# Block-summary scores of an attention stage: two half-width matmuls side by side, or two full-width matmuls that accumulate into one bank

## The chip, the cores and the metric

One core of a Trainium2 chip runs the whole program. The metric is the time of one execution on the device, in microseconds (us). Each kernel was executed several times, and medians are quoted. A ratio is the mean time of one kernel's fast runs over that of the other's fast runs of the same rounds, so it is not quite the ratio of the medians. The granted clock is the share of TensorE's full clock that a run was given. A run counts as slow when it is over 1.5% above the fastest of the same kernel.

## The reference, cut to what matters

An attention stage (4 batches, 8 heads, 768 positions, 64 per head) is followed by a mixture of experts, which takes most of the time. In the attention, each query sees its near keys and, besides, one summary per block of 32 keys, the elementwise maximum of the block:

```python
k_sum = k.reshape(B, H, nb, block, D).max(axis=3)        # nb = 24 blocks
scores_s = scale * np.einsum('bhsd,bhnd->bhsn', q, k_sum)
scores_s = scores_s + np.log(block)
...
a = np.exp(scores_all)
```

The change concerns `scores_s`, a small product: 24 summaries against 768 queries, contraction 64.

## The kernel before: what the change and the argument touch

The kernel works on two heads at a time (a "pair of heads", 16 in all, numbered `i`). Two heads of 64 fill the 128 rows of the matmul array. The maxima of both heads are laid out block-diagonally in `ksT`, so that one matmul gives the summaries of both heads: 64 output partitions (2 heads, 24 blocks padded to 32). As 768 queries don't fit one of the kernel's banks of 512 columns, the queries come in two halves of 384. For the last twelve pairs of heads, both halves go into one bank, one to partitions 0 to 63 and one to 64 to 127:

```python
def key_max_split(i):                      # maxima of both heads, block-diagonal
    nc.vector.tensor_tensor(out=ksT[r][:, 0:64]..., in0=ks[r]..., in1=own..., op=ALU.mult)

def summaries_2(i):
    r, ss = i % NB, bank("a", "ss")
    for h in range(2):                     # h: half of the queries
        at["ss", i, h] = ss[64 * h:64 * h + 64]
        nc.tensor.matmul(ss[64 * h:64 * h + 64, 0:HS], lhsT=ksT[r][:, 0:64],
                         rhs=qT[r][:, W + h * HS:W + (h + 1) * HS], start=True, stop=True)

def summary_exp(i, h):                     # ScalarE, one exponential for each half
    ...
# in the constants, on VectorE, once for each of the four ksT:
nc.vector.memset(t[:, 64:128], 0.0)
```

A planner in the program decides the order of all work on each engine from estimated costs. It fills the attention of later batches with the dense layers of expert 0 (`hps` is its hidden layer, `yps` its output), so that TensorE (PE) always has something to do. Below, "the pair" means the two matmuls of `summaries_2`. Other names in the timelines: `sg` are the scores with the near keys (matmuls of 64 rows), `Ee` the exponentials of the summaries' scores, `av` the attention's result and "the values" the matmuls of line 441 that use `Ee`; `tkq` are transposed queries and keys, `tx` and `xT` the attention's result transposed for the experts, and `lp` the logits of the router that weighs the experts. PEld is TensorE's weight load, DVE is VectorE, ACT is ScalarE.

The softmax here doesn't subtract the row's maximum and nothing guards it: scores larger than these inputs give would overflow.

## Time and profile before

| | |
|---|---|
| time, median of the 6 runs beside the changed kernel | 667.33 us (667.11 to 668.03) |
| span of the profiled execution | 665.9 us |
| TensorE busy | 658.1 us (99%) |
| pairs changed | 12, from 37.0 to 107.1 us |
| from one `hps` matmul's start to the next, 384 columns | 162.5 ns |
| from the pair's first start to the next matmul's start | 286 ns |

The prediction below shows the views. One thing in reading them matters throughout: a matmul's duration in the profile (350 ns here) is longer than the time to the next one's start (162.5 ns in an undisturbed run of the same width), so successive matmuls overlap. What a matmul costs a busy TensorE is the time from its start to the next one's start. I therefore read the single records of the trace for starts in nanoseconds, where a timeline row merges several.

### The profile page before, as it was taken

How to read it: one execution, taken by the hardware profiler on the slowest of the kernel's cores; microseconds unless marked ns; L12 is line 12 of the kernel's file. 1: busy time of each engine (PE TensorE's matmuls, PEld its weight loads, DVE VectorE, ACT ScalarE, POOL GpSimd, SP SyncE). 2: the span in 40 equal slices, each digit the busy share in tenths (PEclk: the TensorE clock that was granted, in tenths of full speed). 3: DMA queues.
4: the chain of work that ended last, by engine and by line, in shares of the span. 5: the costliest groups of instructions: out<-in, count | busy, mean ns of one | idle time of the engine just before them, and what ended most of it. 6: DMA issues, size and time to landing. Idle time of an engine off the chain costs nothing.

```text
span 665.9 us, 13246 instructions
## 1 busy us (share of the span) xinstructions
PE 658.1 (99%) x5132; PEld 434.5 (65%) x5132; DVE 550.3 (83%) x1034; ACT 411.8 (62%) x769; POOL 199.0 (30%) x257
## 2 busy tenths in 40 slices
PE   8999999999999999999999999999999999999997
PEld 4666656555676666666666666666666666666666
DVE  7899977798989887887779877888778877988776
ACT  6677766566875566556665665555655656556652
POOL 8999522100132222212322222213122213222123
PEclk9999999999999999999999999999999999999999
DMA  9999952700763747373754666373838465334656
GB/s 168 183 148 144 136 70 42 127 0 2 134 118 62 123 75 123 66 127 65 110 97 72 119 88 104 64 127 65 127 64 138 69 95 96 64 64 111 155 135 202
DMA packets 112558, 67.89 MB, mean 102 GB/s; under 512 B 77936, under 2 KB 90480, under 8 KB 112496
## 3 DMA queue, kind: packets, MB, share of 16 engines
q0 software_dynamic: 94816, 57.46, 65.3%
q1 hardware_dynamic: 17152, 9.58, 6.2%
q8 instruction: 40, 0.66, 0.4%
q14 instruction: 22, 0.18, 0.1%
q10 hardware_dynamic: 528, 0.02, 0.0%
HBM read 52.45 MB, written 6.29 MB: 88 GB/s over the span
## 4 chain that ended last, share of the span: by engine, by line
PE 93%; DMA 3%; issue 1%; DVE 1%; POOL 0%; ACT 0%; POOLq 0%; DVEq 0%; ACTq 0%
PE yps L815 21%; PE pA L764 21%; PE pY L815 16%; PE pQ L764 10%; PE hps L211 6%; PE yps L216 6%; PE pR L764 5%; DMA out_acc<-y 2%; PE sg L347 1%; PE tkq L303 1%; DMA qst<-in_q_dram 1%; PE vs L357 1%; PE av L435 1%; PE av L512 1%; PE tx L550 1%
## 5 line engine op out<-in xcount | busy, mean ns | idle before, releaser
L815 PEld LDWEIGHTS <-h 128*128 128x128 f16 x2352 | 230.1, 98 | 89.9 <-issue 2.0
L843 POOL DMA_DIRECT2D out_acc<-y x120 | 101.4, 888 | 373.0 <-ACT y L839 107.0
L839 ACT ACTIVATE y<-pY,P_sb 128x256 f32<-128x256 f32 x168 | 80.0, 477 | 126.7 <-PE pY L815 124.0
L830 DVE SCALAR_TENSOR_TENSOR out_acc<-yps,P_sb,out_acc 128x512 f32<-128x512 f32 x128 | 95.3, 745 | 28.0 <-PE yps L815 27.9
L798 DVE TENSOR_TENSOR h<-h 128x1024 f16<-128x1024 f16 x168 | 109.2, 684 | 1.3
L815 PE MATMUL pY<-w,h 128*128 128x256 f16 x672 | 100.3, 273 | 0.6 <-ACT y L839 0.6
L764 PE MATMUL pA<-xT,w 128*128 128x512 f16 x336 | 98.6, 379 | 0.0
L815 PE MATMUL yps<-w2sum,h 128*128 128x256 f16 x672 | 97.9, 273 | 0.0
L815 PE MATMUL yps<-w,h 128*128 128x256 f16 x672 | 93.3, 273 | 0.0
L830 DVE SCALAR_TENSOR_TENSOR out_acc<-pY,P_sb,out_acc 128x512 f32<-128x512 f32 x84 | 62.9, 749 | 29.7 <-PE pY L815 28.1
L764 PEld LDWEIGHTS <-w 128*128 128x128 f16 x672 | 65.8, 98 | 31.3 <-issue 0.2
L764 PEld LDWEIGHTS <-w1sum 128*128 128x128 f16 x504 | 49.3, 98 | 44.6
L786 DVE CUSTOM_DVE_ANT_0 h<-pQ,snap 128x512 f16<-128x512 f32 x84 | 57.7, 686 | 6.5 <-ACT snap L207 3.6
L786 DVE CUSTOM_DVE_ANT_0 h<-pA,snap 128x512 f16<-128x512 f32 x84 | 57.5, 684 | 5.4 <-PE pA L764 5.0
L202 ACT ACTIVATE h<-pA 128x512 f16<-128x512 f32 x84 | 50.6, 603 | 12.1 <-PE pA L764 12.0
L202 ACT ACTIVATE h<-pR 128x512 f16<-128x512 f32 x84 | 50.1, 596 | 8.1 <-PE pR L764 8.1
L815 PE MATMUL pY<-w2sum,h 128*128 128x256 f16 x336 | 50.4, 273 | 0.6 <-ACT y L839 0.5
L207 ACT COPY pR<-pA 128x512 f32<-128x512 f32 x82 | 46.8, 571 | 6.7 <-PE pA L764 5.9
L764 PE MATMUL pA<-xsum,w 128*128 128x512 f16 x168 | 50.0, 379 | 0.0
L764 PE MATMUL pQ<-xsum,w1sum 128*128 128x512 f16 x168 | 50.0, 379 | 0.0
L764 PE MATMUL pR<-xT,w 128*128 128x512 f16 x168 | 50.0, 379 | 0.0
L764 PE MATMUL pQ<-xT,w1sum 128*128 128x512 f16 x168 | 50.0, 379 | 0.0
(150 smaller groups left out, 851.6 us busy)
## 6 DMA issues: line engine op xcount, KB each, us to landing
out_acc<-y POOLq DMA_DIRECT2D x120, 256.0 KB, 3.4
w<-in_moe_w_dram POOLq DMA_DIRECT2D x14, 1024.0 KB, 10.3
out_dram<-out_acc SPq DMA_DIRECT2D x24, 256.0 KB, 2.4
qst<-in_q_dram POOLq DMA_DIRECT2D x32, 96.0 KB, 5.6
vx<-in_v_dram POOLq DMA_DIRECT2D x15, 192.0 KB, 6.4
kst<-in_k_dram POOLq DMA_DIRECT2D x24, 96.0 KB, 5.7
w<-in_moe_w_dram POOLq DMA_DIRECT2D x4, 256.0 KB, 7.0
w<-in_moe_w_dram POOLq DMA_DIRECT2D x2, 512.0 KB, 8.5
```

What stands on the lines that cost most here:

```text
L202: nc.scalar.activation(out=out, in_=in_, func=AF.Relu, bias=0.0, scale=1.0)
L207: (nc.scalar.copy if eng == "ACT" else nc.vector.tensor_copy)(out=out, in_=in_)
L211: nc.tensor.matmul(hp[:, 0:n], lhsT=w1s[e][:, dk, f * 128:(f + 1) * 128], rhs=xT[:, dk, t0:t0 + n], start=(dk == 0), stop=(dk == KD - 1))
L216: nc.tensor.matmul(yp[:, d], lhsT=h[:, f, c * 128:(c + 1) * 128], rhs=w2s[e][:, f, d], start=(f == 0), stop=(f == KF - 1))
L303: nc.tensor.transpose(t[:, g * 128:(g + 1) * 128], st[:, g, :, :].rearrange("p j d -> p (j d)"), ident)
L764: nc.tensor.matmul(dst[:], lhsT=lhsT, rhs=rhs, start=first and k == 0, stop=k == HK - 1, skip_group_check=True)
L786: nc.vector._custom_dve(dve_ops.TENSOR_ADD_SAT, out=ring(e, p, q)[:, q % 2, blk, :], in0=at[src, e, p, q][:], in1=at.pop(("snap", n, e, p, ...
L798: nc.vector.tensor_tensor(out=h[:, :, out_, :], in0=h[:, :, a, :], in1=h[:, :, b, :], op=op)
L815: nc.tensor.matmul(dst[:, d], lhsT=lhsT, rhs=rhs, start=f == 0 and n in (1, 5, 2), stop=f == HF - 1, skip_group_check=True)
L830: nc.vector.scalar_tensor_tensor(out=o, in0=y, scalar=scalar, in1=o, op0=ALU.mult, op1=ALU.add)
L839: nc.scalar.activation(out=at[key][:, d], in_=src, func=AF.Copy, bias=0.0, scale=P_sb[:, t, e:e + 1])
L843: nc.gpsimd.dma_start(out=o, in_=at.pop(("y", e, p, c, key))[:], accum_op=ALU.add)
```

## The change

Its intent: the two narrow matmuls become full-width ones, so that the array never changes its shape for them. `ksT` becomes 192 columns wide, with zeros on both sides of the 64 columns of maxima. The window 64:192 has the maxima first and zeros after, and the window 0:128 has the zeros first. The first matmul puts half 0 on partitions 0 to 63 and zeros on the others. The second adds zeros to those and half 1 to the others.

```diff
-        ksT = [attn.tile([128, 128], BF16, name=f"ksT{i}") for i in range(NB)]
+        ksT = [attn.tile([128, 192], BF16, name=f"ksT{i}") for i in range(NB)]
...
-            nc.vector.tensor_tensor(out=ksT[r][:, 0:64].rearrange("p (j n) -> p j n", j=2),
+            nc.vector.tensor_tensor(out=ksT[r][:, 64:128].rearrange("p (j n) -> p j n", j=2),
...
-            nc.tensor.matmul(ss[:, 0:HS], lhsT=ksT[r][:], rhs=rhs, start=True, stop=True)
+            nc.tensor.matmul(ss[:, 0:HS], lhsT=ksT[r][:, 64:192], rhs=rhs, start=True, stop=True)
...
-                nc.tensor.matmul(ss[64 * h:64 * h + 64, 0:HS], lhsT=ksT[r][:, 0:64],
-                                 rhs=qT[r][:, W + h * HS:W + (h + 1) * HS], start=True, stop=True)
+                nc.tensor.matmul(ss[:, 0:HS], lhsT=ksT[r][:, 64 - 64 * h:192 - 64 * h],
+                                 rhs=qT[r][:, W + h * HS:W + (h + 1) * HS], start=h == 0, stop=h == 1)
...
-                nc.vector.memset(t[:, 64:128], 0.0)
+                nc.vector.memset(t[:], 0.0)
```

The order of instructions stays the same on every engine.

## The prediction

> **What bounds the kernel now.** I read the page first: its busy shares, then the chain that ended last.
>
> ```profile
> PE 658.1 (99%) x5132; PEld 434.5 (65%) x5132; DVE 550.3 (83%) x1034; ACT 411.8 (62%) x769; POOL 199.0 (30%) x257
> ...
> PE 93%; DMA 3%; issue 1%; DVE 1%; POOL 0%; ACT 0%; POOLq 0%; DVEq 0%; ACTq 0%
> ```
>
> TensorE (PE) is busy for 99% of the span and holds 93% of the chain. A busy matmul row is no proof of a full array, because matmuls overlap, so I next asked for the table of stretches and for all waits of PE.
>
> ```profile
> 36.00:72.00 36.00, 36.00 (x454) 23.48 (x451) 33.53 (x89) 28.04 (x45) 35.24 (x42) 1.00 2.36 145
> 72.00:110.00 38.00, 38.00 (x375) 22.48 (x374) 31.15 (x86) 28.79 (x54) 12.73 (x23) 1.00 0.96 83
> ...
> PE pY L815 <- ACT y L839: 1.0, 2, 0.6
> PE tkq L312 <- DMA qst<-in_q_dram: 0.7, 1, 0.7
> ```
>
> The columns of the first two lines are the stretch, its length, then busy us of PE, PEld, DVE, ACT and POOL, the granted clock (1.00, full), and DMA. The changed matmuls (line 461) run from 37.0 to 107.1 us, so both stretches hold all of them: PE never stops there, and its list of waits for them is empty. The waits shown lie before 8 us or after 554 us. In this region the order on PE sets the end: time taken out of PE's stream is time off the kernel, as long as no new wait appears.
>
> The two matmuls themselves, by tile, and then in the timeline of PE around one pair:
>
> ```profile
> L461 PE MATMUL ss<-qT,ksT x24: 350/350/350, 37.0 to 107.1; 128*64 128x384 bf16 x24
> L472 ACT ACTIVATE Ee<-ss x24: 471/487/488, 37.4 to 108.4; 64x384 bf16<-64x384 f32 x24
> ...
> 45.56 0.82 PE L211 MATMUL hps<-xT,w 128*128 128x384 f16 x4
> 46.32 0.35 PE L461 MATMUL ss<-qT,ksT 128*64 128x384 bf16 x2
> 46.60 0.82 PE L211 MATMUL hps<-xT,w 128*128 128x384 f16 x4
> ```
>
> The third line from the end is a run of four full-width matmuls of 384 columns, the second the pair. Its two matmuls take 0.35 us together although each takes 350 ns: in the single records the second starts 4 ns after the first. Each uses half of the array's columns (128\*64), and the halves run side by side. So the pair already costs one matmul's streaming, not two. What matters are its edges: 46.60 - 46.32 = 0.28 us until the next matmul starts. In an undisturbed run of the same width the chain of waits shows
>
> ```profile
> 115.77 1.95 PE hps L211 x12
> ```
>
> that is 1.95 / 12 = 0.1625 us each. The excess is the subject of this prediction.
>
> **What the Trainium skill says.** "TensorEngine Tiling (Array Packing)", section Key Properties: different tiles work in parallel, and changing the tiling mode drains TensorE. The trace agrees on both. I listed, for each change of line on PE, the time from one matmul's start to the next beyond its own streaming. Full-width to full-width: 0 (hps to tkq, yps to av and others), with waits on semaphores or not. Full-width to the 64-column pair: 93 to 94 ns, ten times of ten. Pair to full-width: 286 ns after the pair's first start, against 162.5, so 120 ns beyond the 4 ns of stagger, twelve of twelve. "TensorE: Matmul & The Clock Gate", section Back-to-back issue gap: N/2.4 + 2.5 ns for N columns at full clock; for 384 that is 162.5, which the line above shows exactly. Its section Weight-path perf modes says the fast weight load needs 128 columns; the trace has 106 ns for the 64-column load and 98 ns for a 128-column one, both hidden under streaming, so I give this no weight. "Perfetto Trace Analysis", section Tensor Engine Instruction: PE's end times are modelled; hence I count from start to start.
>
> **The change part by part.** There are twelve pairs (24 matmuls). Their instructions stay in number and order on every engine: the comparison of instruction orders differs only in 24 matmul shapes (64 to 128 columns) and four memsets.
>
> 1. *Removed: the mode switch in, the narrow pair, the switch out.* For a pair behind a full-width matmul (ten of twelve): 94 + 286 = 380 ns until the next matmul starts, and that next one then holds PE 173 ns in place of 162.5, so 11 more: 391 ns.
> 2. *Added: two full-width matmuls one after the other.* They are written to all 128 partitions of one bank and the second adds to the first, as the four hps matmuls of a group do without a gap. 2 x 162.5 = 325 ns. The zero half of the weights costs nothing in itself. Saved: 391 - 325 = 66 ns, ten times, 0.66 us.
> 3. *Two pairs come behind score matmuls of 64 rows* (sg; at 53.8 and 107.1 us). There a switch is paid whatever follows: 90 ns into the pair, 92 to 93 into full width. Before: 90 + 286 + 11 = 387. After: 92 + 325 + 11 = 428. Lost: 41 ns twice, 0.08 us. No pair is followed by a tiled matmul.
> 4. *The maxima* are written to columns 64 to 127 in place of 0 to 63, same shape (216 ns, sixteen times): zero. The h=1 matmuls of the first batch (line 455) read the same 128 columns shifted: zero.
> 5. *Memsets*: four of 128x32 words, at a step of about 42 ns, become 128x96. From 128x64 at a step of 75 ns I estimate about 108, so 0.27 us more on DVE at 2 us. DVE then waits 1.09 us for a load before 7.01 us, so this hides.
>
> Sum on PE: 0.08 - 0.66 = **-0.58 us**, under 0.1% of 667.41. After 110 us nothing is changed, so I carry it to the end unreduced: 666.83.
>
> **The rivals.**
>
> *The lost concurrency is what counts.* If the switches were not real (a modelled record), the pair would cost 162.5 and become 325: +162.5 ns x 12 = +1.95 us, 669.4. Against it: start-to-start times are not modelled ends, and the same 94 ns stands at every change of shape into tiled matmuls.
>
> *A new wait on ACT.* The exponentials wait for the second matmul. Counted from the point where PE gets to the pair, that matmul ended at 94 + 354 = 448 ns and will end near 162.5 + 326 = 488, so 40 ns later, and PE gets to the values 66 ns earlier: 106 ns of slack go. Behind sg it is 444 against 92 + 162.5 + 337 = 591, some 150 ns later. If every pair passed 106 to 150 ns on to PE, that would give back up to about 1.4 us: 668.2. Against it: the slack from the end of an exponential to the matmuls that use it is 0.54 us at least over the twelve pairs (each half has its own), and in all but two pairs ACT was still busy with something else 0.1 to 1.2 us after the matmul ended. So I expect no share of this.
>
> *The gain is swallowed later.* PE waits at 180, 555 and 660 us (0.3 to 0.7 us each) for y, and the chain goes through two transfers of out_acc at 538 and 551 us. If these came from something fixed in time, PE would only wait longer: 667.4. Their issues follow PE's own progress, so I expect the shift to pass; their times vary, which is most of my range.
>
> **Range and chances.** The centre is 666.8; I round the small risk of the last two rivals in and say **666.9 us**. The three runs before spread from 667.11 to 668.03, wider than the effect, so the range is set by noise of about half a microsecond and an error of about 0.3 in the sum: **666.1 to 667.7**. A change of 2% would be 13.3 us; the twelve pairs occupy 12 x 0.39 = 4.7 us altogether, so faster by over 2% has 0.003, slower by over 2% 0.007, within 2% 0.99.
>
> **What would show each step right or wrong.** Line 461 should read 128\*128, with durations of about 326 ns and the second start 162.5 ns behind the first; the matmul before it should hold PE for its own streaming only, and the next should start 325 ns after the first of the pair (336 behind sg). PE's list of waits between 36 and 110 us should stay empty, and the start of the last product stage near 660 us should come about 0.6 us sooner. The prediction is wrong if full-width summaries show an edge of their own (waits for their semaphores exposed, a gap between two matmuls that accumulate), if values (line 441) begin to wait for Ee, or if the tail's transfers move by more than the effect.

## The result, and the profile after

The changed kernel took 667.17 us (median of 6 runs, 666.70 to 668.20) against 667.33 us before. The ratio of the fast runs is 0.9998, with a 95% interval from 0.9985 to 1.0011: the same. That lies in the predicted range, but so would an unchanged 667.33, and the time alone can't tell 0.58 us from zero. The trace can.

First the page of the changed kernel, its busy line and its chain:

```profile
PE 658.5 (99%) x5132; PEld 436.2 (66%) x5132; DVE 550.4 (83%) x1034; ACT 411.4 (62%) x769; POOL 198.8 (30%) x257
...
PE 95%; DVE 2%; DMA 1%; POOL 1%; issue 0%; ACT 0%; POOLq 0%; DVEq 0%
```

Nothing of the change is to be seen at this level: PE busy even reads 0.4 us more, and the larger share of PE in the chain comes mainly from the two transfers of `out_acc` that the chain before had led through near 540 us and this one does not. Next the pair by its tile, and the timeline of PE around the same pair as before:

```profile
L461 PE MATMUL ss<-qT,ksT x24: 323/326/337, 37.8 to 107.7; 128*128 128x384 bf16 x24
L472 ACT ACTIVATE Ee<-ss x24: 472/487/490, 38.4 to 108.8; 64x384 bf16<-64x384 f32 x24
...
46.48 0.82 PE L211 MATMUL hps<-xT,w 128*128 128x384 f16 x4
47.14 0.49 PE L461 MATMUL ss<-qT,ksT 128*128 128x384 bf16 x2
47.46 0.81 PE L211 MATMUL hps<-xT,w 128*128 128x384 f16 x4
```

The columns of a timeline row are start, length (both us), engine, line, operation, tiles, rows\*columns of the array in use, shape and count. Read the starts. The four `hps` matmuls in front lead to the pair after 47.14 - 46.48 = 0.66 us, where it was 46.32 - 45.56 = 0.76 before: the switch into the narrow shape is gone. The pair itself now holds PE for 47.46 - 47.14 = 0.32 us, where it was 0.28. It got dearer by itself and cheaper with its edges.

The order of matmuls is the same in both kernels (5132 of them), so each can be matched with its counterpart. For each pair I took, from the single records, the time that it and its two edges hold PE: from the start of the matmul in front to the start of the second matmul behind, less the streaming of the one in front and the one behind (N/2.4 + 2.5 ns for N columns, the formula that the prediction cites; undisturbed runs here give 56, 162.5 and 216 ns for 128, 384 and 512 columns).

| pair behind | count | before, ns | after, ns | predicted before, after |
|---|---|---|---|---|
| full-width matmuls | 10 | 388 to 392 | 325 to 326 | 391, 325 |
| score matmuls of 64 rows | 2 | 385, 387 | 428, 428 | 387, 428 |
| sum over the twelve | 12 | 4671 | 4108 | |

So the pairs save 4671 - 4108 = 563 ns, where the prediction had 10 x 66 - 2 x 41 = 578.

What a switch consists of is a separate question, and the records show something here that the prediction read wrongly. The first pair with its weight loads, before and then after:

```profile
37.03 0.11 PEld L461 LDWEIGHTS <-ksT 128*64 128x64 bf16 x2 [0.42 <-DVE em L412]
37.04 0.35 PE L461 MATMUL ss<-qT,ksT 128*64 128x384 bf16 x2
...
37.62 0.31 PEld L461 LDWEIGHTS <-ksT 128*128 128x128 bf16 x2
37.83 0.49 PE L461 MATMUL ss<-qT,ksT 128*128 128x384 bf16 x2
```

In all twelve narrow pairs the first load starts only 1 to 2 ns before its matmul, and the load of the full-width matmul behind only 4 to 5 ns before that one. In the changed kernel, behind a full-width matmul, the pair's first load starts 54 to 214 ns ahead, while the matmul in front still streams; behind a score matmul of 64 rows it is 4 ns again. So at a change of shape the load (95 to 106 ns) does not start ahead. Whether the 94 and 120 ns are the array running empty or this load, no run here tells apart; the sums are measured from start to start and hold either way.

The rest of the difference between the two profiled executions is not time of the pairs. Three other things happened. They add 0.39 us together, so that the spans, 665.9 and 665.8 us, lie only 0.15 us apart.

The start of the changed kernel came 0.89 us later. Its complete list of waits of PE shows two waits for transfers that the first trace of before did not have:

```profile
PE idle L613 <- DVE zeros L632: 1.3, 1, 1.3
PE pY L815 <- ACT y L839: 0.6, 1, 0.6
PE vs L357 <- DMA vx<-in_v_dram: 0.4, 1, 0.4
PE hps L211 <- DMA w<-in_moe_w_dram: 0.3, 1, 0.3
```

In the timelines of PE, first of the kernel before and then of the changed one, the first hidden matmuls of expert 0 show it:

```profile
18.36 0.66 PE L211 MATMUL hps<-xT,w 128*128 128x384 f16 x3
```

```profile
17.66 0.52 PE L357 MATMUL vs<-vx,m_blk 128*128 128x128 bf16 x6 [0.43 <-DMA vx<-in_v_dram]
...
19.25 0.66 PE L211 MATMUL hps<-xT,w 128*128 128x384 f16 x3 [0.34 <-DMA w<-in_moe_w_dram]
```

What stands in brackets is the idle time in front and what ended it. These matmuls run 18 us before the first changed pair. On the other side, the execution before had a wait near 555 us, long after the last pair, which the changed one lacks (first before, then the same place after):

```profile
554.97 0.60 PE L815 MATMUL pY<-w2sum,h 128*128 128x256 f16 x4 [0.48 <-ACT y L839]
```

```profile
554.81 0.60 PE L815 MATMUL pY<-w2sum,h 128*128 128x256 f16 x4
```

The matched starts show 648 ns of difference arising at this single matmul. The third thing is small: two short waits of PE between 37 and 67 us grew by 90 and 61 ns. The 61 ns one turned out to belong to the change; the 90 ns one is at a transposition of `qst` at 38.58 us, in front of which the trace shows a semaphore wait of PE's sequencer. The second trace of the changed kernel doesn't have the 90 ns, so it isn't inherent in the change; its cause I leave open.

Whether the start and the wait near 555 us belong to the kernels or to the single execution was the first question for the experiments.

### The profile page after: what moved, and what is told of

It is laid out like the page before. It is cut to its first block, busy times and chain, and to the rows that moved or that the text cites. A ratio compares the mean times of both kernels' runs of the same rounds, so it can differ in the third digit from the quotient of the medians.

```text
span 665.8 us, 13247 instructions
## 1 busy us (share of the span) xinstructions
PE 658.5 (99%) x5132; PEld 436.2 (66%) x5132; DVE 550.4 (83%) x1034; ACT 411.4 (62%) x769; POOL 198.8 (30%) x257
## 4 chain that ended last, share of the span: by engine, by line
PE 95%; DVE 2%; DMA 1%; POOL 1%; issue 0%; ACT 0%; POOLq 0%; DVEq 0%
PE yps L815 22%; PE pA L764 22%; PE pY L815 17%; PE pQ L764 11%; PE hps L211 6%; PE yps L216 6%; PE pR L764 5%; DMA w<-in_moe_w_dram 1%; PE sg L347 1%; PE tkq L303 1%; PE av L435 1%; PE av L512 1%; PE ss L461 1%; PE vs L357 1%; PE av L441 1%; PE tx L550 1%
## 5 line engine op out<-in xcount | busy, mean ns | idle before, releaser
L764 PE MATMUL pA<-xsum,w1sum 128*128 128x512 f16 x168 | 50.0, 379 | 0.0
```

Of the source, the lines that this page charges most:

```text
L764: nc.tensor.matmul(dst[:], lhsT=lhsT, rhs=rhs, start=first and k == 0, stop=k == HK - 1, skip_group_check=True)
```

## The experiments

**A measure without the start.** In each trace I took the time from the start of the first hidden matmul of expert 0 (18.4 us, after the loads that vary) to the start of the last matmul. It excludes the start. A trace with the wait near 555 us has 0.65 us more, and only the first trace of the kernel before has it. The theories:

- *Theory S*: the mode switches around the narrow pair cost what the starts say, and taking them out shortens PE's stream.
- *Rival N*: nothing on the path changes. *Rival C*: the switches are not real, and the loss of concurrency is what counts. *Rival M*: the longer memsets push the start. *Theory D and rival A* concern the 61 ns and come below.

### The changed kernel again

No edit.

> The changed kernel once more, to measure the change with less noise. Theory S (mode switches): twelve pairs save 0.57 us on TensorE, of which the wait of the logits for a copy on VectorE near 66 us takes back 0.07, so 0.50 us less than before, ratio 0.9992. Theory N (nothing changes on the path): 1.0000. In the trace theory S expects full-width to pair 162 to 163 ns, pair to next 325, and the logits' wait near 66 us again some 210 ns long, against 149 before. The start (the v load before 18 us) shows whether the 0.9 us later start of the first trace of the changed kernel comes back: if it is the loads' own spread, it need not.

Measured: 667.27 us (5 runs, 667.17 to 667.68) against 667.31 (11 runs of before); ratio 0.9994 (0.9982 to 1.0006): the same, and the interval holds both the expected 0.9992 and 1. In the trace the pairs sum to 4107 ns, the logits' wait is 208 ns, and the first hidden matmul came at 19.09 us, late again. The time without the start is 641.95 us.

### Only the wider tile and memsets

```diff
# kernel before
-        ksT = [attn.tile([128, 128], BF16, ...
+        ksT = [attn.tile([128, 192], BF16, ...
...
-            nc.tensor.matmul(ss[:, 0:HS], lhsT=ksT[r][:], rhs=rhs, start=True, stop=True)
+            nc.tensor.matmul(ss[:, 0:HS], lhsT=ksT[r][:, 0:128], rhs=rhs, start=True, stop=True)
...
-                nc.vector.memset(t[:, 64:128], 0.0)
+                nc.vector.memset(t[:], 0.0)
```

> The kernel before with only the wider tile and the wider memsets of the change; narrow pairs stay. Theory S: the 0.27 us on VectorE hide, time as before within 0.1 us, TensorE start of expert 0 near 18.4 us. Rival M: the longer memsets push the start; then the first hidden matmul of expert 0 starts 0.3 to 0.9 us later than 18.36 and the time is 0.3 to 0.9 us longer.

Measured: 667.31 us (667.13 to 667.69), ratio 0.9995 (0.9983 to 1.0007). The pairs sum to 4671 ns as before; the first hidden matmul is at 18.67 us, 0.3 later. By the letter that is the low end of the start that rival M expects, though the time is not 0.3 us longer, so this run alone doesn't decide; the table below does as far as it goes.

### Wide pairs, except behind the score matmuls

```diff
# changed kernel
+                rhs = qT[r][:, W + h * HS:W + (h + 1) * HS]
+                if i in (6, 15):
+                    nc.tensor.matmul(ss[64 * h:64 * h + 64, 0:HS], lhsT=ksT[r][:, 64:128], rhs=rhs,
+                                     start=True, stop=True)
+                    continue
```

> As the change, but the two pairs behind score matmuls of 64 rows (near 54 and 107 us) stay narrow. Theory S: they return to 387 ns from 428, 0.08 us less than the changed kernel in all (ratio to before 0.9991), too small to see in the time but to be read in the trace: 90 ns into the pair, 286 out of it at these two, 0 and 325 at the other ten.

> Wide pairs except behind score matmuls, once more, for the time: theory S 0.58 us less than before (ratio 0.9991); theory N 1.0000. In the trace the pairs sum to 4.02 us against 4.67, and the logits' wait near 66 us is some 210 ns.

The timeline of PE around the first of the two pairs left narrow (line 463 in this kernel is the narrow matmul, as lines have moved):

```profile
53.36 0.38 PE L347 MATMUL sg<-qT,kT 64*128 64x160 bf16 x6
53.67 0.35 PE L463 MATMUL ss<-qT,ksT 128*64 128x384 bf16 x2
53.96 0.51 PE L303 MATMUL tkq<-ident,kst 128*128 128x128 bf16 x6
```

The two cost 386 and 387 ns, the other ten 324 to 326; together 4024 ns in both traces, as expected. The times: 667.11 us (6 runs, 666.50 to 670.91), ratio 1.0003 (0.9983 to 1.0023), and in the second round of runs 668.29 (5 runs, 666.72 to 668.57) against 667.65, ratio 1.0000 (0.9987 to 1.0014). Neither time confirms the 0.58 us. The two traces show what hides it: one starts its first hidden matmul at 18.36 us, the other at 20.32, in one and the same kernel, and the times of these two executions are 666.50 and 668.57 us; the time without the start is 641.86 and 641.87.

### The pair six times over, narrow and wide

To lift the effect out of the spread, each pair is issued six times, with a full-width matmul between the repeats. All write the same bank, and the last pair leaves the right result, so both kernels are correct. The edit in the kernel before (in the changed kernel it is the same around the wide pair, with columns 64:192):

```diff
+            for n in range(6):
+                if n:
+                    nc.tensor.matmul(ss[:, 0:HS], lhsT=ksT[r][:, 0:128], rhs=qT[r][:, W:W + HS],
+                                     start=True, stop=True)
                 for h in range(2):
                     nc.tensor.matmul(ss[64 * h:64 * h + 64, 0:HS], lhsT=ksT[r][:, 0:64], ...
```

> The kernel before with each narrow pair issued six times, a full-width matmul of 384 columns between the repeats (all write the same bank; the last pair leaves the right result). Theory S (each visit to the narrow pair costs 94 ns in, 286 to the next start, 11 more in that one): 5 x (391 + 162.5) ns x 12 = 33.2 us more than before, about 700.5 us. Rival C (the switches are not real, a pair costs one streaming time): 5 x (166 + 162.5) x 12 = 19.7 us more, about 687.

> The changed kernel with each full-width pair issued six times, a full-width matmul between, as in the other. Theory S: 5 x (325 + 162.5) ns x 12 = 29.25 us more than the changed kernel, about 28.7 more than before, 696.1 us; 4.5 us less than the same with narrow pairs. Rival C: the wide one is the dearer, by 5 x 159 ns x 12 = 9.5 us and more.

Measured: narrow 701.38 us (700.27 to 702.86), wide 696.64 us (695.93 to 696.79), before 667.27. Theory S expected 700.5 and 696.1; rival C expected 687 for the narrow one and the wide one dearer. Here the time itself decides: the narrow kernel is the slower by 4.7 us, clear of the spread. One repeat in the timeline of PE, narrow first (line 466 is the pair, 463 the matmul between):

```profile
38.27 0.34 PE L463 MATMUL ss<-qT,ksT 128*128 128x384 bf16 x1
38.54 0.35 PE L466 MATMUL ss<-qT,ksT 128*64 128x384 bf16 x2
38.82 0.34 PE L463 MATMUL ss<-qT,ksT 128*128 128x384 bf16 x1
```

```profile
37.42 0.33 PE L463 MATMUL ss<-qT,ksT 128*128 128x384 bf16 x1
37.58 0.49 PE L466 MATMUL ss<-qT,ksT 128*128 128x384 bf16 x2
37.91 0.33 PE L463 MATMUL ss<-qT,ksT 128*128 128x384 bf16 x1
```

A round of pair and one full-width matmul takes 38.82 - 38.27 = 0.55 us narrow and 37.91 - 37.42 = 0.49 us wide. The full-width matmul between takes 0.27 us from its start to the narrow pair and 0.16 to the wide one. Over all twelve places the stretches grew by 33.13 us (narrow, predicted 33.2) and by 29.25 us (wide, predicted 29.25). Rival C falls. The times lie 0.9 and 0.5 us above the expectation. The traces show what can be in it: first hidden matmuls at 19.32 and 18.52 us instead of 18.35, and two waits for `y` near 370 and 440 us (0.14 and 0.16 us narrow, 0.21 and 0.41 us wide) that no kernel with single pairs shows. From the first hidden matmul to the last, less these two waits, the traces have 675.56 and 671.12 us: 4.44 us apart, where 33.13 - 29.25 us for the repeats and 0.56 us for the first pairs also make 4.44.

### The kernel before, a second trace

> The kernel before, unchanged, for a second trace. If the late start of the changed kernel (first hidden matmul at 19.1 to 19.3 us against 18.37) and the 0.65 us wait near 555 us, which only the first trace of the kernel before shows, are spread between executions, then this trace need not repeat 18.37 and need not have the wait; if they belong to the kernels it repeats both. Pairs again 385 to 392 ns each.

The first hidden matmul is at 18.35 us again, but the wait near 555 us is not there; the timeline of PE at that place:

```profile
554.09 0.38 PE L764 MATMUL pA<-xT,w 128*128 128x512 f16 x1
554.30 0.60 PE L815 MATMUL pY<-w2sum,h 128*128 128x256 f16 x4
```

So that wait belonged to one execution. The time without the start is 642.43 us, and this is the figure to compare with.

### One copy moved from VectorE to ScalarE

In the traces with one narrow pair each (before, before again, only memsets), the logits (line 570) of the second batch wait 144 to 151 ns near 66 us; in those with one wide pair each 204 to 211. The list of waits leaves out waits this short; they stand only in the starts. The timelines of VectorE (DVE) and of PE there, before:

```profile
64.83 0.48 DVE L367 COPY Ve<-Ve 64x650 bf16<-64x650 bf16 x1
65.24 0.54 DVE L412 TENSOR_TENSOR em<-er,band 128x768 bf16<-128x768 bf16 x1
65.71 0.54 DVE L207 COPY xT<-tx 128x768 f16<-128x768 f16 x1
...
65.82 0.50 PE L303 MATMUL tkq<-ident,qst 128*128 128x128 bf16 x6
66.30 0.74 PE L570 MATMUL lp<-wg_bf,xT 128*128 128x8 f16 x24
```

and after:

```profile
66.60 0.54 DVE L207 COPY xT<-tx 128x768 f16<-128x768 f16 x1
...
66.66 0.50 PE L303 MATMUL tkq<-ident,qst 128*128 128x128 bf16 x6
67.20 0.74 PE L570 MATMUL lp<-wg_bf,xT 128*128 128x8 f16 x24
```

The logits wait for the copy of `tx` into `xT`, which ends at 65.71 + 0.54 = 66.25 in the kernel before. From the last row of transposes to the logits it is 0.48 us before and 0.54 after. In the changed kernel that copy, and every instruction of VectorE from 60 us up to it, came 0.89 to 0.90 us later than before, just as the start did, while PE and ScalarE had gained 65 ns from the pair at 60 us. VectorE runs through this stretch, up to that copy, with pauses of at most 35 ns, so I suspected that it sets the time there (theory D).

```diff
-                nc.vector.tensor_copy(out=ve[0:64, 1:G, :],
-                                      in_=ve[0:64, 0:1, :].to_broadcast([64, G - 1, 2 * VD]))
+                (nc.scalar.copy if i == 9 else nc.vector.tensor_copy)(
+                    out=ve[0:64, 1:G, :], in_=ve[0:64, 0:1, :].to_broadcast([64, G - 1, 2 * VD]))
```

> The kernel before with one 0.48 us copy (the block sums of pair 9 into Ve, near 64.8 us) moved from VectorE to ScalarE. Theory D: VectorE, busy without a pause from 60 to 66.25 us, sets the logits' wait near 66 us; with the copy gone its chain ends some 0.45 us earlier and the 149 ns wait is 0. Rival A: the wait comes from ScalarE or a transfer; then it stays at 149 ns or grows, since ScalarE has more to do. Time within its own spread either way.

> The changed kernel with the same copy moved. Theory D: the logits' wait near 66 us, 210 ns in the changed kernel, is 0, so that the saving of the pair at 60 us (66 ns) is no longer given back: the twelve pairs together and all that follows gain 0.56 us against the narrow kernel with the same move. Rival A: the wait stays 60 ns longer than in that one.

The wait did not go to 0, as I had expected: it is 143 ns narrow and 142 ns wide. But the extra of the wide version is gone, and the reason for the remainder can be read in the timeline of VectorE, narrow first:

```profile
65.19 0.54 DVE L412 TENSOR_TENSOR em<-er,band 128x768 bf16<-128x768 bf16 x1
66.14 0.56 DVE L207 COPY xT<-tx 128x768 f16<-128x768 f16 x1 [0.42 <-PE tx L550]
```

```profile
64.62 0.54 DVE L412 TENSOR_TENSOR em<-er,band 128x768 bf16<-128x768 bf16 x1
65.53 0.56 DVE L207 COPY xT<-tx 128x768 f16<-128x768 f16 x1 [0.37 <-PE tx L550]
```

Now the copy waits for PE's transposes (line 550), which it did not before. From PE's last transpose to the logits there is a round trip over the copy, and the work that PE has meanwhile (twelve more transposes) is 143 ns too short to cover it. That is the floor of this wait, and it moves with PE. In the kernel before, VectorE's chain ended only some 6 to 8 ns later than this floor (149 and 151 ns in its two traces): it was as good as balanced, and any gain of PE in front of it turned into waiting. Theory D holds for what the change lost, and my expectation of 0 was wrong about the base. Each was a single execution (667.46 and 666.73 us, state unknown). The time without the start is 642.43 us narrow and 641.89 us wide: a gain of 0.55 us, nearly the 0.56 us that the twelve pairs save.

### Both together

The wide pairs except behind score matmuls, with the one copy moved.

> Wide pairs except behind score matmuls, and the one copy of pair 9 moved to ScalarE: the best version that the experiments point to. Theory S with D: from the first hidden matmul to the last matmul 642.44 us (kernel before, second trace) minus 0.65, so 641.79; the kernel's time some 0.65 us less than before when the start is the same (ratio 0.9990), which the spread of the start (0 to 2 us between executions) can hide.

Measured: 641.81 us without the start, 0.63 less than before (expected 641.79). The time: 666.91 us (5 runs, 666.55 to 668.99) against 667.49 (9 runs); ratio 0.9998 (0.9985 to 1.0012). It is ahead of both kernels in the trace, and by the time the same.

### The traces side by side

| kernel, trace | first hidden matmul, us | from there to the last matmul, us | twelve pairs, ns |
|---|---|---|---|
| before | 18.37 | 643.08 (wait near 555 us) | 4671 |
| before, second trace | 18.35 | 642.43 | 4672 |
| only wider memsets | 18.67 | 642.44 | 4671 |
| before, copy moved | 18.83 | 642.43 | 4667 |
| changed | 19.25 | 642.04 | 4108 |
| changed again | 19.09 | 641.95 | 4107 |
| changed, copy moved | 18.35 | 641.89 | 4107 |
| wide except behind scores | 18.36 | 641.86 | 4024 |
| the same, second trace | 20.32 | 641.87 | 4024 |
| the same, copy moved | 18.36 | 641.81 | 4023 |

The last two columns go together to within 0.09 us, once the wait near 555 us and the 90 ns of the first changed trace are taken off. The start in the first column of figures does not follow the kernel. The wide memsets occur with starts from 18.35 to 20.32 us, the narrow ones from 18.35 to 18.83, and 19.32 in the sixfold narrow kernel. So a start at 18.35 is possible with the wide memsets, and a late one without them; rival M, as a fixed delay, falls. Whether the wide memsets make a late start a little more frequent, ten traces and their spread can't say; this stays open.

## Why the prediction was right

The time (667.17 us) fell inside 666.1 to 667.7, and "within 2%" was right. That is weak support: the range was set by the noise, and an unchanged time lies in it too. In the first pair of profiles the sizes agree partly by luck, since a late start (0.89 us) and a missing wait (0.65 us) happened to offset each other. What bears the prediction out are the starts. By its steps:

- **What bounds the kernel.** PE's stream sets the end in this region: of the 565 ns saved at the pairs (4672 - 4107, the second trace of each kernel), 480 arrived at the last matmul (642.43 - 641.95).
- **Step 1, the switches.** The size was right: 388 to 392 ns for 391, and confirmed in the time by the sixfold kernels. Its reading of the weight loads, "both hidden under streaming", was wrong: at every change of shape the load starts with its matmul (1 to 5 ns before it). So that the switch is a drain, with which the prediction saw the trace agree, is not shown here; only its cost is.
- **Step 2, two wide matmuls.** Right to the nanosecond: 325. Accumulating into the same bank costs no gap.
- **Step 3, pairs behind score matmuls.** Right: 428 ns for 428. Leaving these two narrow saves 83 ns more.
- **Step 4, shifted columns.** Nothing to be seen of it, as predicted.
- **Step 5, memsets.** The size was right: the instruction behind them starts at 2.49 us instead of 2.22, 0.27 later. They hide: VectorE still waits 0.76 us for its load before it goes on at 6.96 us.
- **The rival "lost concurrency".** Rightly rejected; the sixfold kernels show it.
- **The rival "a new wait on ACT".** The values did not begin to wait, as predicted. (Its 150 ns behind score matmuls should have been 106: the matmul ends 147 ns later there, but PE reaches the values 41 ns later too.) But I looked for slack only there. This is the step that failed in part: "so I carry it to the end unreduced". PE already had a wait of 149 ns at the logits near 66 us, which my own list of starts contained and which I didn't follow. VectorE's chain was within 8 ns of setting it, and took back 61 ns in the first pair of traces and 57 in the second. So the net gain is 0.48 us and not 0.58; some 25 ns more went in steps of at most a few ns all along the stream, which I did not trace.
- **"PE never stops there, and its list of waits for them is empty."** Too strong: that list leaves out waits as short as these. Besides the 149 ns, the starts before have one of 76 ns at 43.81 us; it stayed at 75 to 81 ns in every trace.
- **"The gain is swallowed later."** Not so: beyond 110 us the offset between matched matmuls stays constant to 2 ns, but for the one wait near 555 us of one execution.
- **"The last product stage near 660 us about 0.6 us sooner."** In the first pair of traces it came only 0.15 us sooner (660.25 to 660.10), for the three other reasons above. As a test on a single trace this was badly chosen.

## What to carry to other kernels

Two narrow matmuls side by side need not be cheaper than two wide ones, if each visit to the narrow shape pays for a switch in and out (388 to 392 ns against 325 here, at 384 columns): add the edges, start to start, to the streaming time, and look at the shape of the neighbours, since behind another tiled matmul the balance turns (385 to 387 ns against 428). When a change is smaller than the spread of the executions, repeat its subject several times inside the kernel, or measure an interval in the trace that leaves the varying part out. Before you carry a gain to the end, look at every wait that the bound engine already has behind it, short ones too, and ask which other engine is about to set it.

## What the Trainium skill lacked or had wrong

- "TensorEngine Tiling (Array Packing)", Key Properties, says that changing the tiling mode drains TensorE and gives no price. Here it is 93 to 94 ns from full width into the 64-column pair, 90 from the 64-row mode into it, 120 out of it into full width, 92 to 93 from the 64-row mode into full width, and some 11 ns more in the first matmul of the full-width mode. Nor does a page say that at such a change the first weight load starts only with its matmul: 1 to 5 ns ahead here, against 54 to 214 for the wide pair between full-width matmuls.
- The same page's table under Theoretical Speedup counts by the tiles alone (up to 2x for a dimension of 64), without the edges of a visit. In this kernel, two tiles side by side with one visit cost 388 to 392 ns where two full-width matmuls cost 325.
- "TensorE: Matmul & The Clock Gate", Back-to-back issue gap, says that a real stream of weight loads and matmuls runs at about 81 ns per matmul at N=128 and about 131 at N=512, and calls N/2.4 + 2.5 the isolated case. Here streams with a load for each matmul run at 56 ns (128 columns), 162.5 (384) and 216 (512), which is that formula. The point concerns that section alone.
- "Perfetto Trace Analysis" has nothing on the spread between executions of one kernel: here the first hidden matmul behind the loads came between 18.35 and 20.32 us, and a wait of 0.65 us near 555 us in one trace of the twelve taken.
